# Top-k attention with a mixture of depths: the mask of each score tile is added by TensorE during the transpose, not by ScalarE and GpSimd ahead of it

## The chip, the cores and the metric

The kernel runs on one core of one Trainium2 chip. The metric is device time in microseconds (us) of one execution; smaller is better. A core has five engines that run their own queues in order and wait for each other by semaphores: PE (TensorE, matrix products; PEld is its loading of weights), DVE (VectorE), ACT (ScalarE), POOL (GpSimd) and SP, which here issues DMAs.

## The reference

For 8 batches and 8 heads, with 576 tokens and a head size of 64, attention keeps for each query the 32 largest scores of its 576, takes the softmax over them, and multiplies by the values. The result (8 x 576 x 512) goes through a mixture of depths: per batch a gate scores each token, and the 128 best tokens get a two-layer network added, scaled by a sigmoid.

```
scores = scale * np.matmul(q, k.transpose(0, 1, 3, 2))
kth = np.partition(scores, -top_k, axis=-1)[..., -top_k:-top_k + 1]
mask = scores >= kth
scores = np.where(mask, scores, -1000000000.0)
attn = np.exp(scores - max); attn = attn / (sum + 1e-09)
attn_out = np.matmul(attn, v)
...
top_idx = np.argpartition(-gate_scores[b], capacity)[:capacity]
out[b, top_idx] = x[b, top_idx] + sigmoid(gate)[:, None] * (relu(xe @ w1) @ w2)
```

## The kernel before

**Units and tiles.** The work is cut into 160 units: 8 batches, 5 blocks of queries (four of 128 rows, one of 64), 4 pairs of heads. A unit of a full block has two score tiles of 128 x 576, one for each head; a unit of the short block packs both heads into one tile. So each batch has 20 units and 36 tiles, and the run has 288 tiles.

**The pipeline.** One loop runs over steps n, one step for each unit, and a unit passes through six steps. In step n the engines do, for different units:

- PE: `turn` and `turn_last` of unit n-3 (transposes of the masked scores: four chunks of 128 x 128 for each tile, into the PSUM tile `ptr`, and one for the last 64 keys of both heads, into a corner of the score tile `ps`), between them `values` of unit n-4 (products with v into `av`), then `multiply` of unit n+1 (scores into `ps`), then a piece of the mixture of the batch before (`h_ps`, `y_ps`, `extra_ps`) or of loading the next batch (`tr`).
- DVE: `find_bound` of unit n (`cand`, `best`: a bound from the maxima of eight slices), then `find_kth` of unit n-1 (`next8`, shown as `next`: its element 7 is the 32nd largest score), then `gates` (`prod`) and parts of the mixture (`junk`, `sig`, `pick`).
- ACT: `part` of unit n-1 (`sides`, the sign of score minus bound), the exponentials of unit n-3 (`pT`, `last`), copies that were put off (`flush`), the first half of the mask of unit n-2 (`z`), `keep` of unit n+1 (`sc`, the scores copied out of PSUM), `keep_values` (`xs`), `cut` (the CAST to `seen`).
- POOL: `y` = score times side for unit n-1, `fill`, the second half of the mask of unit n-2 (`z`), once for each block of queries the normalisation `x`, and `lift` (`seen`, 2^90 times the 32nd largest score).

**Masking.** ACT makes z = relu(2^90 * (kth - score)) and POOL makes z = score - z, so that a score below the limit becomes hugely negative and its exponential is zero. Both are done for every tile:

```
act.activation(
    z[:, i, :],
    sc[:, i, :],
    AF.Relu,
    bias=seen[:, 1, at + i : at + i + 1],
    scale=-BIG,
)
pool.tensor_tensor(z[:, i, :], sc[:, i, :], z[:, i, :], ALU.subtract)
```

**What sets the order.** The order within each engine is that of the program, fixed by `InOrder` (its line, L42, is what the profile shows for all these instructions, so groups are told apart by their tiles). `ps` and `av` have one buffer each: `multiply` waits until ACT has read `last` from the corner of the same `ps`, and `values` waits until `keep_values` has emptied `av`. The masked tile `z` has two buffers, the scores `sc` four.

Of the kernel before, what the change touches and what calls it, by code (L numbers as in the profile page):

```python
# [20 lines left out]
BIG = 2.0**90  # L21
# [4 lines left out]
LEAST = 1.0e-16 * SMALLER  # L26
# [19 lines left out]
def kernel(  # L46
# [11 lines left out]
    nc = tc.nc  # L58
# [6 lines left out]
    JP = J * P  # L65
# [34 lines left out]
    slot = const.tile([P, CAP], FP32, name="slot")  # L100
    nc.vector.tensor_copy(out=slot, in_=slot_i)


# [239 lines left out]

    def lift(n, next8, at):
        pool.tensor_scalar_mul(seen[:, 1, at : at + n], next8[:, 0:n, 7], BIG)

    def turn(i, z):

        tr = ps_tr.tile([P, 512], FP32, name="ptr")
        for c in range(J):  # L350
            at = c * P + i * R
            pe.transpose(tr[:, c * P : (c + 1) * P], z[:, i, at : at + P], ident)
        return tr

    def turn_last(n, z, ps):

        last = z.rearrange("p i s -> p (i s)")[:, JP : JP + n * R]  # L360
        tr = ps[0 : n * R, 1, 1, 512 - P : 512]
        pe.transpose(tr, last, ident)
        return tr
# [91 lines left out]
    def break_ties(t, gate, gate_row, rank):  # L455

        n = R if t == J else P
        work = wkpool.tile([P, 2, S], FP32, name="ties", tag="z")
        tok_row = modpool.tile([P, S], I32, name="tok_row", tag="scratch")
# [183 lines left out]
    load_at = (1, 2, 3, 4, 7, 8, 9, 11, 12)  # L643
    first_load_at = (5, 6, 7, 8, 9, 10, 11, 12, 13)
    v_at = 6
    mix_from = 5
    first_tile, tiles = [], 0
# [10 lines left out]
    xs = x = gate = None  # L658
    scs, bests, zs, weights = {}, {}, {}, {}

    def tiles_of(n):
        return len(heads_of(units[n][1])) if 0 <= n < len(units) else 0

    for n in range(-1, len(units) + 6):
# [19 lines left out]
        for i in range(2):  # L684
            if i < tiles_of(n - 3):
                trs.append(turn(i, z))
                if i == tiles_of(n - 3) - 1:
                    trs.append(turn_last(i + 1, z, ps))
            if i < tiles_of(n - 4):
                values(t4, hp4, i, *weights[n - 4], av, qkv[b4][2])  # L690
# [6 lines left out]
        if tiles_of(n - 1):  # L697
# [21 lines left out]
        if tiles_of(n + 1):  # L719
            b, t, hp = units[n + 1]  # L720
            multiply(t, hp, *qkv[b][0:2], ps)


        if tiles_of(n - 2):
            sc = scs.pop(n - 2)
            z = wkpool.tile([P, 2, S], FP32, name="z")
            at = first_tile[n - 2]
            for i in range(tiles_of(n - 2)):
                act.activation(
                    z[:, i, :],  # L730
                    sc[:, i, :],
                    AF.Relu,
                    bias=seen[:, 1, at + i : at + i + 1],
                    scale=-BIG,
                )
# [15 lines left out]
        if gating is not None:  # L751
# [6 lines left out]
        b, i = divmod(n, per_batch)  # L758
        if i >= mix_from or b > 0:
            next(mixing, None)  # L760
        if normalising is not None:
# [9 lines left out]
        if tiles_of(n - 1):  # L771
            lift(tiles_of(n - 1), next8, first_tile[n - 1])
        b, i = divmod(n, per_batch)
        if n >= 0 and b + 1 < B:
            steps_of_load = first_load_at if b == 0 else load_at
            if i == steps_of_load[0] - 1:
                qkv[b + 1] = room_for_qkv(b + 1)
                loading = load_kq(k[b + 1], q[b + 1], *qkv[b + 1][0:2])
                next(loading)
            if i in steps_of_load:  # L780
                next(loading)
            if i == v_at:
                load_v(v[b + 1], qkv[b + 1][2])

# [7 lines left out]
    for what, op, than, limit in (  # L792
        (seen[:, 0, :], ALU.min, ALU.is_gt, LEAST),
        (seen[:, 1, :], ALU.min, ALU.is_gt, LEAST * BIG),
        (seen[:, 2, :], ALU.max, ALU.is_lt, float(MIDDLE)),
# [28 lines left out]
    def general_weights(n, sc):  # L824

        p = wkpool.tile([P, 2, S], FP32, name="p", tag="z")
        for i in range(n):
            cur, tops = sc[:, i, :], []
            left = wkpool.tile([P, 2, S], FP32, name="left", tag="z")
            for r in range(TOP_K // 8):  # L830
# [99 lines left out]
```

## Time and profile before

| | us |
|---|---|
| median of 3 runs | 1170.49 |
| lowest and highest of them | 1162.18, 1174.98 |
| the profiled execution | 1161.06 |
| its span in the trace | 1158.6 |

| engine | busy us | share of the span |
|---|---|---|
| PE | 985.9 | 85% |
| DVE | 910.0 | 79% |
| POOL | 905.8 | 78% |
| ACT | 879.7 | 76% |

The mean granted clock of PE is 0.878 of full speed. The four engines are nearly equally busy, so the shares alone say little; the sections below go by steps. Steps are counted here within a batch of 20, from 0 to 19, and a step is taken from one CAST of `cut` on ACT to the next. Batches are counted from 0; batch 4 lasts from 557.41 to 697.24 us.

### The profile page before, as it was taken

What the parts mean: (1) busy time and instruction counts of PE and PEld (TensorE: products, weight loads), DVE (VectorE), ACT (ScalarE), POOL (GpSimd) and SP (SyncE); (2) the same over time, 40 slices, a digit from 0 to 9 for tenths busy, and PEclk for the clock granted to TensorE, in tenths of its full rate; (3) what the DMA queues carried; (4) which work ended last, traced back from release to release, by engine and by line L of the source; (5) the groups of instructions that cost most, each with busy time, mean ns of one, the idle gap of its engine ahead of it and who ended that gap; (6) DMA issues with size and microseconds to landing.
All of it is one profiled execution on the core that took longest, in us unless ns stands there. A gap on an engine that the chain in (4) does not pass through costs nothing.

```text
span 1158.6 us, 23113 instructions
## 1 busy us (share of the span) xinstructions
PE 985.9 (85%) x6906; PEld 820.3 (71%) x6906; DVE 910.0 (79%) x4980; ACT 879.7 (76%) x2113; POOL 905.8 (78%) x974
## 2 busy tenths in 40 slices
PE   6788878899789988899888998889987898778946
PEld 3566657787677876778677786678766787667845
DVE  5888788787897778976898868978789777898640
ACT  4898798696978769777786878969797876978721
POOL 3999798797978769777787878879797887878820
PEclk9898897799977989779886899969998788978978
DMA  5641022100411013110141101410041001000020
GB/s 121 199 100 28 1 80 63 36 2 11 114 38 29 1 17 108 38 28 1 21 114 28 28 1 34 119 28 11 9 110 26 10 1 47 5 1 10 1 60 13
DMA packets 123829, 49.03 MB, mean 42 GB/s; under 512 B 118960, under 2 KB 118960, under 8 KB 122672
## 3 DMA queue, kind: packets, MB, share of 16 engines
q1 hardware_dynamic: 120320, 42.88, 14.4%
q0 software_dynamic: 1792, 4.20, 2.1%
q8 instruction: 58, 0.95, 0.3%
q14 instruction: 75, 0.61, 0.2%
q10 hardware_dynamic: 1584, 0.39, 0.2%
HBM read 35.91 MB, written 11.53 MB: 41 GB/s over the span
## 4 chain that ended last, share of the span: by engine, by line
PE 51%; ACT 20%; POOL 19%; DVE 5%; issue 4%; DMA 1%; POOLq 0%; ACTq 0%
PE av L42 18%; PE ps L42 13%; POOL y L42 9%; PE ptr L42 9%; POOL z L42 8%; PE h_ps L42 6%; ACT sides L42 6%; ACT sc L42 5%; PE y_ps L42 4%; ACT pT L42 3%; ACT z L42 3%; PE extra_ps L42 2%; DVE prod L42 1%; DVE next L42 1%; POOL out_dram L607 1%
## 5 line engine op out<-in xcount | busy, mean ns | idle before, releaser
L42 POOL TENSOR_TENSOR z<-sc,z 128x576 f32<-128x576 f32 x288 | 407.7, 1434 | 62.9 <-ACT z L42 61.9
L42 POOL TENSOR_TENSOR y<-sc,sides 128x576 f32<-128x576 f32 x288 | 363.0, 1279 | 116.9 <-ACT sides L42 109.1
L42 DVE MAX8 cand<-sc 128x8 f32<-128x72 f32 x2304 | 323.5, 216 | 89.9 <-ACT sc L42 89.4
L42 PE MATMUL av<-v,pT 128*128 128x65 f32 (+1 forms) x2560 | 340.9, 283 | 5.5 <-ACT xs L42 5.2
L42 PEld LDWEIGHTS av<-v,pT 128*128 128x128 f32 (+1 forms) x2560 | 324.2, 203 | 18.4 <-ACT xs L42 10.2
L42 PE MATMUL ptr<-ident,z 128*128 128x128 f32 x1152 | 206.5, 308 | 113.7 <-POOL z L42 113.7
L42 DVE MAX8 next<-y 128x8 f32<-128x584 f32 x288 | 207.8, 759 | 98.9 <-POOL y L42 97.6
L42 PE MATMUL ps<-kT,qT 64*128 64x288 f32 (+1 forms) x1280 | 232.4, 488 | 21.3 <-ACT last L42 16.6
L42 ACT COPY sc<-ps 128x576 f32<-128x576 f32 x288 | 171.7, 647 | 99.6 <-PE ps L42 99.5
L42 PEld LDWEIGHTS ptr<-ident,z 128*128 128x128 f32 x1152 | 146.0, 159 | 142.4 <-POOL z L42 139.1
L42 ACT ACTIVATE pT<-ptr 128x512 f32<-128x512 f32 x288 | 163.0, 585 | 88.4 <-PE ptr L42 87.8
L42 ACT ACTIVATE sides<-sc,seen 128x576 bf16<-128x576 f32 x288 | 221.1, 768 | 4.9
L42 ACT ACTIVATE z<-sc,seen 128x576 f32<-128x576 f32 x288 | 210.5, 783 | 1.4 <-POOL seen L42 1.4
L42 PEld LDWEIGHTS ps<-kT,qT 64*128 64x128 f32 (+1 forms) x1280 | 119.5, 203 | 73.2 <-ACT last L42 30.2
L42 DVE MAX8 best<-cand 128x8 f32<-128x64 f32 x864 | 154.2, 215 | 3.3
L42 DVE MATCH_REPLACE8 cand<-best,cand 128x64 f32<-128x64 f32 x576 | 116.5, 209 | 0.0
L42 PEld LDWEIGHTS h_ps<-xeT,w 128*128 128x128 f32 x512 | 64.7, 205 | 16.6 <-issue 11.8
L42 DVE CUSTOM_DVE_ANT_0 prod<-x,wg 128x512 f32<-128x512 f32 (+1 forms) x40 | 72.1, 1802 | 4.5 <-POOL x L42 4.5
L42 PE MATMUL h_ps<-xeT,w 128*128 128x128 f32 x512 | 70.9, 296 | 2.1 <-ACT hT L42 1.4
L42 PE MATMUL y_ps<-w,hT 128*128 128x192 f32 (+1 forms) x384 | 62.2, 315 | 1.5 <-ACT gy L42 1.1
L42 PE MATMUL av<-vpair,last 128*128 128x130 f32 x256 | 63.4, 333 | 0.0
L42 PEld LDWEIGHTS y_ps<-w,hT 128*128 128x128 f32 x384 | 56.1, 190 | 10.1 <-issue 7.7
(74 smaller groups left out, 859.3 us busy)
## 6 DMA issues: line engine op xcount, KB each, us to landing
rows<-in_k_dram SPq DMA_DIRECT2D x64, 128.0 KB, 2.8
v<-in_v_dram SPq DMA_DIRECT2D x64, 128.0 KB, 3.0
out_dram<-x SPq DMA_DIRECT2D x8, 1024.0 KB, 4.7
rows<-in_q_dram SPq DMA_DIRECT2D x62, 128.0 KB, 2.9
w<-in_moe_w_dram SPq DMA_DIRECT2D x2, 2048.0 KB, 14.0
last<-in_k_dram SPq DMA_DIRECT2D x8, 128.0 KB, 3.1
vlast<-in_v_dram SPq DMA_DIRECT2D x8, 128.0 KB, 3.7
vpair<-in_v_dram SPq DMA_DIRECT2D x16, 64.0 KB, 3.1
```

Of the source, the lines that this page charges most:

```text
L42: return lambda *a, **kw: self._tc.keep_in_program_order(fn(*a, **kw))
L607: nc.gpsimd.indirect_dma_start(out=out.flatten_outer_dims(), out_offset=bass.IndirectOffsetOnAxis(ap=row_i, axis=0), in_=gy, in_offset=Non ...
```

## The change

The scores themselves are now transposed, without a mask. After each transpose of a 128 x 128 chunk, TensorE adds to the same place in PSUM the product of a bf16 mask chunk `less` and a constant matrix `out_of_reach` (the identity times -2^90). `less` is positive (or 1) where a score lies below the 32nd largest and 0 elsewhere. Of the two tiles of a unit, ACT makes the mask of the first (a Relu) and POOL that of the second (a comparison); both read the limit from `next8`. `lift`, the product with 2^90, is gone; POOL copies the limits into `seen` for the check at the end. The scores must live longer, so `sc` has five buffers. The table of load steps is written in another form, for the same steps.

```diff
-    scpool = ctx.enter_context(tc.tile_pool(name="sc", bufs=4))
+    scpool = ctx.enter_context(tc.tile_pool(name="sc", bufs=5))
...
+    out_of_reach = const.tile([P, P], BF16, name="out_of_reach")
+    nc.vector.tensor_scalar_mul(out_of_reach, ident, -BIG)
...
-    def lift(n, next8, at):
-        pool.tensor_scalar_mul(seen[:, 1, at : at + n], next8[:, 0:n, 7], BIG)
-
-    def turn(i, z):
+    def mask(n, sc, next8):
+
+        less = wkpool.tile([P, 2, S], BF16, name="less")
+        for i in range(n):
+            kth = next8[:, i, 7:8]
+            if i == 0:
+                act.activation(less[:, i, :], sc[:, i, :], AF.Relu, bias=kth, scale=-1.0)
+            else:
+                pool.tensor_scalar(
+                    out=less[:, i, :],
+                    in0=sc[:, i, :],
+                    scalar1=kth,
+                    scalar2=None,
+                    op0=ALU.is_lt,
+                )
+        return less
+
+    def turn_some(tr, z, less):
+
+        pe.transpose(tr, z, ident)
+        if less is not None:
+            pe.matmul(
+                tr, less, out_of_reach, start=False, stop=True, skip_group_check=True
+            )
...
-            next8 = find_kth(tiles_of(n - 1), y)
+            next8s[n - 1] = find_kth(tiles_of(n - 1), y)
...
-            z = wkpool.tile([P, 2, S], FP32, name="z")
-            at = first_tile[n - 2]
-            for i in range(tiles_of(n - 2)):
-                act.activation(
...
-                pool.tensor_tensor(z[:, i, :], sc[:, i, :], z[:, i, :], ALU.subtract)
-            zs[n - 2] = z
+            w, at = tiles_of(n - 2), first_tile[n - 2]
+            kth = next8s.pop(n - 2)
+            masks[n - 2] = mask(w, scs[n - 2], kth)
+            pool.tensor_copy(out=seen[:, 1, at : at + w], in_=kth[:, 0:w, 7])
```

The order of the instructions on PE, in a step with full units early in the run. In the kernel before, `ptr` and the first `ps` row are `turn` and `turn_last`, the two `av` rows `values`, the last `ps` row `multiply`:

```order
L42 MATMUL ptr<-ident,z 128x128 x4
L42 MATMUL av<-v_115,pT 128x65 x4
L42 MATMUL ptr<-ident,z 128x128 x4
L42 MATMUL ps<-ident,z 128x128
L42 MATMUL av<-v_115,pT 128x65 x4
L42 MATMUL av<-vpair_119,last 128x130
L42 MATMUL ps<-kT,qT 128x288 x4
```

The transposes stand where they stood; each is now followed by one loading of `less` and one product.

On PE after the change, from the last chunk of the second `turn` of such a step to its `multiply` (the first three rows stand three more times ahead of these):

```order
L42 MATMUL ptr<-ident,sc 128x128
L42 LDWEIGHTS less
L42 MATMUL ptr<-out_of_reach,less 128x128
L42 MATMUL ps<-ident,sc 128x128
L42 LDWEIGHTS less
L42 MATMUL ps<-out_of_reach,less 128x128
L42 MATMUL av<-v_117,pT 128x65 x4
L42 MATMUL av<-vpair_121,last 128x130
L42 MATMUL ps<-kT,qT 128x288 x4
```

A full unit has nine such pairs, a unit of the short block five; none existed before.

On POOL before the change, over a step at whose end a block of queries is normalised (`x`), and into the next:

```order
L42 TENSOR_TENSOR y<-sc,sides 128x576 x2
L42 TENSOR_TENSOR y<-steps,seen 128x2x8
L42 TENSOR_TENSOR z<-sc,z 128x576 x2
L42 TENSOR_TENSOR x<-xs,rden 128x512
L42 TENSOR_SCALAR seen<-next_908 128x2
L42 TENSOR_TENSOR y<-sc,sides 128x576 x2
```

Here `lift` (the `seen` row) stands behind `x`, and the mask of the next step needs it.

On POOL after the change, the same place:

```order
L42 TENSOR_TENSOR y<-sc,sides 128x576 x2
L42 TENSOR_TENSOR y<-steps,seen 128x2x8
L42 TENSOR_SCALAR less<-sc,next_853 128x576
L42 COPY seen<-next_853 128x2
L42 TENSOR_TENSOR x<-xs,rden 128x512
L42 TENSOR_TENSOR y<-sc,sides 128x576 x2
```

Two subtractions became one comparison, and what stands behind `x` is no longer needed by any mask.

## Rows read from the trace of the kernel before

**Rows 1.** The page: POOL's two costliest groups (busy us, mean ns, idle before).

```profile
L42 POOL TENSOR_TENSOR z<-sc,z 128x576 f32<-128x576 f32 x288 | 407.7, 1434 | 62.9 <-ACT z L42 61.9
L42 POOL TENSOR_TENSOR y<-sc,sides 128x576 f32<-128x576 f32 x288 | 363.0, 1279 | 116.9 <-ACT sides L42 109.1
```

**Rows 2.** Stretches of batch 4: length, busy PE, PEld, DVE, ACT, POOL, PEclk, DMA.

```profile
562.84:578.64 15.80, 12.16 (x80) 8.80 (x81) 13.14 (x70) 11.90 (x31) 12.35 (x14) 0.78 0.21 34
578.64:590.47 11.83, 9.93 (x78) 8.09 (x76) 9.38 (x63) 11.77 (x29) 11.44 (x13) 1.00 0.53 165
590.47:605.57 15.10, 12.81 (x78) 10.93 (x79) 15.03 (x75) 11.79 (x30) 13.77 (x15) 0.77 0.33 74
617.41:638.89 21.48, 19.30 (x87) 16.66 (x88) 15.79 (x86) 12.13 (x32) 15.28 (x16) 0.54 0.06 14
650.73:665.80 15.07, 14.42 (x93) 12.38 (x94) 12.85 (x69) 11.63 (x28) 12.09 (x13) 0.77 0.00 1
665.80:690.99 25.19, 25.19 (x204) 22.27 (x203) 15.80 (x73) 18.15 (x45) 19.41 (x23) 1.00 0.01 1
```

**Rows 3.** The same columns: two stretches of batch 5, one of batch 0, whole batches.

```profile
728.96:741.41 12.45, 9.49 (x75) 8.03 (x75) 12.45 (x68) 11.78 (x29) 12.12 (x13) 1.00 0.40 90
788.79:800.68 11.89, 11.25 (x93) 9.87 (x94) 11.89 (x68) 11.41 (x28) 11.56 (x13) 1.00 0.00 0
106.72:124.09 17.37, 16.98 (x74) 13.44 (x74) 10.90 (x54) 10.21 (x25) 13.94 (x15) 0.51 0.00 1
...
143.98:970.55 826.57, 730.99 (x5173) 612.11 (x5172) 676.82 (x3723) 656.77 (x1584) 673.25 (x714) 0.88 0.16 39
970.55:1097.15 126.60, 107.56 (x760) 90.51 (x759) 108.52 (x584) 100.28 (x243) 107.53 (x115) 0.88 0.05 15
```

**Rows 4.** Timeline of one plain step (batch 4, step 3), ACT: start, length, what.

```profile
577.43 1.19 ACT L42 COPY sc<-ps 128x576 f32<-128x576 f32 x2
578.48 0.27 ACT L42 COPY xs<-av 64x130 f32<-64x130 f32 x1
...
581.37 0.27 ACT L42 ACTIVATE last<-ps 128x128 f32<-128x128 f32 x1
...
582.00 1.45 ACT L42 ACTIVATE z<-sc,seen 128x576 f32<-128x576 f32 x2
583.33 0.65 ACT L42 COPY sc<-ps 128x576 f32<-128x576 f32 x1
```

**Rows 5.** The same step: weight loads of PE; its last product, of `multiply`.

```profile
578.42 0.42 PEld L42 LDWEIGHTS ptr<-ident,z 128*128 128x128 f32 x4 [1.04 <-POOL z L42]
578.80 0.97 PEld L42 LDWEIGHTS av<-v,pT 128*128 128x128 f32 x8
579.78 0.42 PEld L42 LDWEIGHTS ptr<-ident,z 128*128 128x128 f32 x4
580.17 0.14 PEld L42 LDWEIGHTS ps<-ident,z 128*128 128x128 f32 x1
580.28 0.97 PEld L42 LDWEIGHTS av<-v,pT 128*128 128x128 f32 x8
581.17 0.30 PEld L42 LDWEIGHTS av<-vpair,last 128*128 128x128 f32 x2
...
581.69 1.24 PE L42 MATMUL ps<-kT,qT 64*128 64x288 f32 x8
```

**Rows 6.** Timeline of batch 4, step 1, and of the tail (1104.27): DVE, PE.

```profile
562.73 2.41 DVE L42 CUSTOM_DVE_ANT_0 prod<-x,wg 128x512 f32<-128x512 f32 x1
...
564.64 1.11 PE L42 MATMUL ptr<-ident,z 128*128 128x128 f32 x4 [2.58 <-POOL z L42]
...
1104.27 0.69 DVE L42 CUSTOM_DVE_ANT_0 prod<-x,wg 128x512 f32<-128x512 f32 x1 [3.27 <-POOL x L42]
```

**Rows 7.** Timeline of batch 4, step 9, ACT.

```profile
620.52 0.20 ACT L42 ACTIVATE sig<-sig 128x4 f32<-128x4 f32 x1 [2.87 <-DVE sig L42]
```

**Rows 8.** Timeline of batch 4, step 2: weight loads of 64 columns.

```profile
572.54 0.54 PEld L42 LDWEIGHTS av<-v,pT 128*64 128x64 f32 x8 [0.53 <-ACT xs L42]
```

More of the change, by code (lines that the diff above doesn't have):

```diff
@@ L342, in find_kth, with turn, turn_last @@
         return next8
-    def lift(n, next8, at):
-        pool.tensor_scalar_mul(seen[:, 1, at : at + n], next8[:, 0:n, 7], BIG)
-    def turn(i, z):
+    def mask(n, sc, next8):
[19 more added lines that the diff above has]
+            )
+    def turn(i, z, less=None):
         tr = ps_tr.tile([P, 512], FP32, name="ptr")
         for c in range(J):
-            at = c * P + i * R
-            pe.transpose(tr[:, c * P : (c + 1) * P], z[:, i, at : at + P], ident)
-        return tr
-    def turn_last(n, z, ps):
-        last = z.rearrange("p i s -> p (i s)")[:, JP : JP + n * R]
+            at = slice(c * P + i * R, (c + 1) * P + i * R)
+            turn_some(
+                tr[:, c * P : (c + 1) * P],
+                z[:, i, at],
+                None if less is None else less[:, i, at],
+            )
+        return tr
+    def turn_last(n, z, ps, less=None):
         tr = ps[0 : n * R, 1, 1, 512 - P : 512]
-        pe.transpose(tr, last, ident)
+        last = [
+            a and a.rearrange("p i s -> p (i s)")[:, JP : JP + n * R] for a in (z, less)
+        ]
+        turn_some(tr, *last)
         return tr
@@ L457, in break_ties @@
         n = R if t == J else P
-        work = wkpool.tile([P, 2, S], FP32, name="ties", tag="z")
+        work = wkpool.tile([P, 2, S], FP32, name="ties", tag="y")
         tok_row = modpool.tile([P, S], I32, name="tok_row", tag="scratch")
@@ L644 @@
     first_load_at = (5, 6, 7, 8, 9, 10, 11, 12, 13)
+    load_steps = {}
+    for b in range(B - 1):
+        at = [b * per_batch + i for i in (load_at if b else first_load_at)]
+        load_steps[at[0] - 1] = b + 1, True
+        load_steps.update({n: (b + 1, False) for n in at})
     v_at = 6
-    mix_from = 5
     first_tile, tiles = [], 0
@@ L658 @@
     xs = x = gate = None
-    scs, bests, zs, weights = {}, {}, {}, {}
+    scs, bests, next8s, masks, weights = {}, {}, {}, {}, {}
     def tiles_of(n):
@@ L685 @@
             if i < tiles_of(n - 3):
-                trs.append(turn(i, z))
+                trs.append(turn(i, sc, less))
                 if i == tiles_of(n - 3) - 1:
-                    trs.append(turn_last(i + 1, z, ps))
+                    trs.append(turn_last(i + 1, sc, ps, less))
             if i < tiles_of(n - 4):
@@ L770 @@
                 normalising = b, t, xs, x, gate
-        if tiles_of(n - 1):
-            lift(tiles_of(n - 1), next8, first_tile[n - 1])
-        b, i = divmod(n, per_batch)
[L774 to L783, printed above, removed]
+        if n in load_steps:
+            b, begin = load_steps[n]
+            if begin:
+                qkv[b] = room_for_qkv(b)
+                loading = load_kq(k[b], q[b], *qkv[b][0:2])
+            next(loading)
+        b, i = divmod(n, per_batch)
+        if i == v_at and b + 1 < B:
+            load_v(v[b + 1], qkv[b + 1][2])
     flush()
@@ L793 @@
         (seen[:, 0, :], ALU.min, ALU.is_gt, LEAST),
-        (seen[:, 1, :], ALU.min, ALU.is_gt, LEAST * BIG),
+        (seen[:, 1, :], ALU.min, ALU.is_gt, LEAST),
         (seen[:, 2, :], ALU.max, ALU.is_lt, float(MIDDLE)),
```

17 lines of the change are left out of this document (4 added, 13 removed).

## The prediction

> **What bounds the kernel now.** I read the page first. Its busy shares are so even that no engine bounds the whole, so I went through batch 4 step by step with the view of busy time by stretch [rows 2]. Four kinds of steps stand out.
>
> Plain steps: steps 3 and 4 take 11.83 us together, and ACT is busy for 11.77 of them, POOL for 11.44 [rows 2] (from 578.64). Steps 7-8 and 11-12 read the same (11.84 each). The timeline says why [rows 4]: from one `keep` (577.43) to the next (583.33) ACT never pauses. POOL is as full, with two `y` and two `z`, 1.28 and 1.43 us each on the mean [rows 1].
>
> PE-full steps: in steps 15 to 18 PE is busy for all of 25.19 us, at a granted clock of 1.00 [rows 2] (from 665.80). There the mixture runs on PE beside attention.
>
> Slow pairs: steps 1-2 (15.80 us), 5-6 (15.10) and 13-14 (15.07), with a mean granted clock of 0.77 to 0.78 [rows 2]. The timeline of step 1 shows the cause [rows 6]: DVE's `prod` takes 2.41 us beside POOL's `z` (0.69 in the tail, where POOL is idle), and PE stands 2.58 us waiting for `z`. After that the clock is at its lower level, and the next products take twice as long. That the work itself doesn't need the time is seen in batch 5, where the same two pairs kept the full clock and took 12.45 and 11.89 [rows 3].
>
> The pair 9-10: 21.48 us, at a clock of 0.54 [rows 2] (from 617.41). Here ACT waits 2.87 us for DVE's `sig` [rows 7] and all else waits for ACT; then PE works through the backlog at half speed.
>
> **Removed.** POOL loses two `z` of 1.43 us for each full unit [rows 1], ACT one of its two (a pair takes 1.45 us with overlap, and from the first one's start to `keep` is 1.33, so one is worth 0.67) [rows 4]. `lift` becomes a copy of the same size, and nobody waits for it. PE's wait for `z` ahead of `turn` (1.04 us even in the plain step [rows 5], 2.58 in the slow one [rows 6]) goes: the first tile's mask comes from ACT, which made it a step earlier, right behind the flushed copy.
>
> **Added on POOL.** One comparison of 128 x 576. No row shows one. It can't be cheaper than nothing, and a two-input `z`, 1.43 us, is the upper end; I take 1.0, since it reads one tensor instead of two. POOL then has about 2.5 for `y`, 1.0, and some 0.5 for small ones: 4.0 in a step of 5.7. PE needs this mask only for its second `turn` of the next step, nearly two microseconds after POOL has it. So either end is hidden; the cover is gone only if POOL is about 1.8 us late.
>
> **Added on PE.** Nine pairs of a load of `less` and a product of 128 columns for a full unit, five for a short one: 128 x 9 + 32 x 5 = 1312. Call the price of one pair x. No row shows a bf16 product. Nearest rows: the fp32 transposes, four in 0.39 us (579.78 to 580.17), so 0.0975 each; products with 128 columns of fp32 weights, eight in 0.97, so 0.121 [rows 5]; with 64 columns, as many bytes as 128 of bf16, eight in 0.54 of loading, 0.068 [rows 8]. Below, I allow half a transpose, 0.049. I take x = 0.08, between the 64-column load and the transpose.
>
> [...]
>
> **What is late next in a plain step.** Two loops remain. Through ACT: `keep` starts, `last` starts 3.94 later (577.43 to 581.37), `multiply` 0.32 after that, and the next `keep` needs all its 1.24 us and a handover of some 0.06: 5.56 [rows 4, 5]. ACT's mask and flushed copy fit beside `multiply`. Through PE: `values` can start 1.37 after `keep` starts, because `xs` must have emptied `av` (578.80); from there to the end of the last `av` load is 2.67 (581.47), then `multiply`, 1.30: 5.34. Five of the nine new pairs lie in this part, the other four in PE's gap before `xs`. So the step takes 5.34 + 5x = 5.74, against 5.92 now.
>
> **The sum for batch 4**, in us, before to after:
> Steps 3-4 and 11-12: 11.83 to 11.5, twice: -0.7.
> Steps 1-2: 15.80 to 11.6, two plain steps, one with only five pairs: -4.2. PE no longer stands still for `z`, so I expect the clock to stay up, and `prod` meets an idle POOL.
> Steps 5-6: 15.10 to 11.6: -3.5. The undisturbed 12.45 was DVE-full [rows 3], with perhaps 0.9 of it `prod` waiting behind POOL (up to 1.7 by [rows 6]).
> Steps 13-14: 15.07 to 12.0: -3.1, from the undisturbed 11.89, less the wait of `prod`, plus nine pairs in a PE-full step.
> Steps 7-8: 11.84 to 12.5: +0.65. DVE has five `junk` products there, which now fall into faster steps.
> Steps 15-18, PE-full: 36 pairs: +2.9. Steps 19 and 0: ten pairs: +0.8.
> Steps 9-10: `sig` stays; about 0.9 less for `prod`, nine pairs at half clock (2x): +0.5.
> Together -6.65, from 139.83 to 133.2.
>
> Batches 1 to 6 take 826.57 now [rows 3], some of them with fewer slow pairs. If each comes to 133.2, that is 799: -27.5. Batch 0 has two steps at half clock, 17.37 us [rows 3], which should become 11.6, and plain steps: -9. Batch 7, 126.60 [rows 3], has three slow pairs, no loading and half of the PE-full steps: -6. In the tail PE waits for three last `z`: -3. Sum -45.5.
>
> The profiled execution took 1161.06, so 1115.5; it was 0.8% below the median of 1170.49, and the forecast on the median's scale is 1115.5 x 1.008 = 1124. In the batches x counts some 123 times (50 in loops, 73 in PE-full and half-clock steps), over the run about 920 times. So 0.01 in x is 9 us, and the gain is gone at x = 0.129.
>
> **Rival 1, still faster: the clock stays up in steps 9-10 too.** PE has more to do in every step and no longer starts that pair with a wait for `z`. Without the half clock the pair would take about 16.9 instead of 22.0, seven times: 36 us less, 1088 on the median's scale. Against it: PE was busy for 19.30 of 21.48 us there and still was at half clock [rows 2], and the stall of ACT for `sig`, which starves PE, remains. [...]
>
> **Rival 2, no gain: the new pairs are dear.** If a bf16 load costs what the fp32 load costs, x = 0.121 [rows 5], 38 us of the gain go: 1153, on the median's scale 1163, within 1% of now. For it: nothing in the trace shows a cheaper load of 128 columns than a transpose. [...]
>
> **Rival 3, slower: the halved clock stays in the slow pairs.** PE's waits may only move, from ahead of `turn` to ahead of `multiply`: `prod`, `junk` and the normalisation keep DVE full there (15.03 of 15.10 us [rows 2]), and PE still waits for `last`. Then each pair keeps its 15 us and pays nine pairs at double price: about 3.9 us back for each of some 20 slow pairs of the run, 78 us: 1194, on the median's scale 1203. It decides from about 12 of the 20. For it: DVE's work is unchanged. Against it: each slow pair begins with a wait for `z`, and that is gone.
>
> **How the numbers follow.** Forecast, 1095 to 1150 (x from 0.05 to 0.0975, on the median's scale): 0.55. Rival 1: 0.17. Rival 2: 0.15. Rival 3: 0.13. The range reaches from a little below rival 1 to above rival 2: 1080 to 1168. About 1% is what a measurement of this kernel can tell from no change. Faster by more: forecast, rival 1 and a part of rival 2, 0.76; within 1%: most of rival 2, 0.11; slower: rival 3, 0.13.
>
> **What would show it.** Right: in a plain step PE goes from `multiply` into `turn` without a wait, and its idle time is ahead of `av`, ended by `xs`; plain steps last 5.7; steps 15 to 18 lengthen to about 28; the clock is 1.00 in steps 1-2, 5-6, 13-14; POOL's busy time falls to about 620 us, ACT's by about 90. The pitch of the pairs in `turn` gives x directly. Wrong: a pitch above 0.12, half clock in the slow pairs, or a `turn` that waits for POOL's `less`.

## The result, and the profile after

The changed kernel takes 1092.52 us (median of 4 runs, 1090.8 to 1094.8), the kernel before 1170.36 (4 runs, 1162.18 to 1174.98): a ratio of 0.9343, 95% interval 0.9288 to 0.9399. The profiled execution took 1090.8 us, its span is 1088.9.

The page: busy time, the chain that ended last, and the groups that answer to [rows 1] (busy us, mean ns, idle before).

```profile
PE 996.2 (91%) x8218; PEld 828.7 (76%) x8218; DVE 854.4 (78%) x4981; ACT 799.8 (73%) x1985; POOL 706.0 (65%) x814
...
PE 69%; ACT 18%; POOL 5%; issue 4%; DVE 3%; DMA 1%; SPq 0%; ACTq 0%; POOLq 0%
...
L42 POOL TENSOR_TENSOR y<-sc,sides 128x576 f32<-128x576 f32 x288 | 363.4, 1280 | 287.8 <-ACT sides L42 287.8
...
L42 PE MATMUL ptr<-out_of_reach,less 128*128 128x128 bf16 x1152 | 220.9, 225 | 13.3 <-POOL less L42 13.3
L42 POOL TENSOR_SCALAR less<-sc,next 128x576 bf16<-128x576 f32 x128 | 220.9, 1726 | 0.0
...
L42 PEld LDWEIGHTS <-less 128*128 128x128 bf16 (+1 forms) x1312 | 141.1, 108 | 19.6 <-POOL less L42 14.9
```

PE is now the busiest engine by a distance, and POOL has become an engine that waits: 287.8 us of idle time ahead of `y`. The mean granted clock rose from 0.878 to 0.942. PE waits for POOL's mask only 13.3 us in the whole run.

Batch 3, by the stretches of [rows 2] (steps 1-2, 3-4, 5-6, 7-8, 9-10, 13-14, 15-18; steps 11-12 read like 5-6), then batches 1 to 6 and batch 7, which answer to [rows 3]. The columns are the same.

```profile
395.41:406.71 11.30, 9.88 (x93) 7.37 (x92) 11.16 (x70) 10.51 (x28) 9.28 (x11) 1.00 0.28 47
406.71:418.19 11.48, 11.13 (x96) 9.27 (x96) 10.24 (x64) 10.68 (x27) 9.68 (x10) 1.00 0.52 165
418.19:429.69 11.50, 10.74 (x93) 8.98 (x93) 11.05 (x68) 10.32 (x27) 9.59 (x12) 1.00 0.46 103
429.69:442.51 12.82, 12.26 (x106) 10.30 (x105) 12.66 (x74) 10.95 (x27) 8.25 (x10) 1.00 0.31 70
442.51:461.75 19.24, 16.41 (x95) 13.39 (x93) 14.88 (x86) 10.75 (x28) 12.31 (x14) 0.65 0.08 16
...
473.25:485.18 11.93, 11.74 (x104) 10.20 (x104) 10.66 (x67) 10.08 (x26) 9.45 (x11) 1.00 0.01 2
485.18:512.94 27.76, 27.76 (x236) 24.26 (x235) 15.08 (x73) 17.00 (x43) 11.99 (x16) 1.00 0.00 1
...
130.68:908.44 777.76, 736.60 (x6150) 617.32 (x6151) 636.00 (x3722) 597.48 (x1489) 523.43 (x594) 0.95 0.17 41
908.44:1029.43 120.99, 110.58 (x919) 92.00 (x918) 100.74 (x584) 89.92 (x226) 84.75 (x95) 0.94 0.06 16
```

The three slow pairs are gone: 1-2, 5-6 and 13-14 have the full clock and last 11.3 to 11.9 us, where batch 4 had 15.07 to 15.80. Steps 15 to 18 pay for it with 2.57 us (25.19 to 27.76). From batch 1 on only the pair 9-10 still has the lower clock, in each of the seven batches; batch 0 has it in steps 1-2 (13.30 us at 0.50). Batches 1 to 6 lost 48.8 us of their 826.57, batch 0 11.8 (124.37 to 112.58, by its step boundaries), batch 7 5.6, and start and tail together 3.5: that is the difference of the spans, 69.7 us.

A plain step of the changed kernel (batch 3, from one `keep` to the next; timeline: start, length, what), to be read beside [rows 4, 5]:

```profile
416.97 1.18 ACT L42 COPY sc<-ps 128x576 f32<-128x576 f32 x2 [0.31 <-PE ps L42]
...
417.34 0.27 PE L42 MATMUL ptr<-ident,sc 128*128 128x128 f32 x1
417.45 0.22 PE L42 MATMUL ptr<-out_of_reach,less 128*128 128x128 bf16 x1
...
417.85 0.28 PE L42 MATMUL ptr<-ident,sc 128*128 128x128 f32 x1
417.96 0.22 PE L42 MATMUL ptr<-out_of_reach,less 128*128 128x128 bf16 x1
418.37 1.11 PE L42 MATMUL av<-v,pT 128*128 128x65 f32 x8 [0.19 <-ACT xs L42]
...
421.44 1.24 PE L42 MATMUL ps<-kT,qT 64*128 64x288 f32 x8
...
422.72 1.18 ACT L42 COPY sc<-ps 128x576 f32<-128x576 f32 x2 [0.31 <-PE tr L42]
```

From `keep` to `values` is 1.40 us, from there to `multiply` 3.07, from there to the next `keep` 1.28: together 5.75. The first and the fourth transpose of `turn` start 0.51 apart, so transpose and pair take 0.17; with the 0.0975 for a transpose of [rows 5] that leaves 0.072 for the pair. The 0.39 us in which [rows 5] has four loads are a little short, since the first of them starts early (0.06 ahead of the second, the others 0.11 apart): two transposes in a row start 0.109 apart (the median in steps 15 to 18 of the kernel before), which leaves 0.061 between them. PE's idle time stands ahead of `av` and ends with `xs`.

The start of step 9 in batch 3 (timeline of POOL, DVE, ACT and PE):

```profile
438.61 0.20 DVE L42 RECIPROCAL rden<-sums 128x8 f32<-128x8 f32 x1
438.90 1.04 POOL L42 TENSOR_TENSOR x<-xs,rden 128x512 f32<-128x512 f32 x1 [3.35 <-DVE rden L42]
...
442.57 1.73 POOL L42 TENSOR_SCALAR less<-sc,next 128x576 bf16<-128x576 f32 x1
...
443.99 0.67 DVE L42 CUSTOM_DVE_ANT_0 prod<-x,wg 128x512 f32<-128x512 f32 x1
...
444.36 0.29 PE L42 MATMUL ptr<-out_of_reach,less 128*128 128x128 bf16 x1 [1.72 <-POOL less L42]
...
444.86 0.21 ACT L42 ACTIVATE sig<-sig 128x4 f32<-128x4 f32 x1 [2.14 <-DVE sig L42]
...
446.39 0.20 ACT L42 ACTIVATE sig<-sig 64x1 f32<-64x1 f32 x1 [1.32 <-DVE sig L42]
...
449.28 2.29 PE L42 MATMUL ps<-kT,qT 64*128 64x288 f32 x8 [1.11 <-ACT last L42]
```

Two stalls follow one another. DVE makes `rden` only behind its `junk` comparisons, POOL holds back `x`, `y` and `less` for it, and PE stands 1.72 us. Then ACT stands 2.14 and 1.32 us for `sig`. The view by stretch says where the clock is in this:

```profile
442.51:443.78 1.27, 0.13 (x2) 0.00 (x0) 1.15 (x2) 0.19 (x1) 1.27 (x2) 1.00 0.62 139
443.78:457.43 13.65, 11.97 (x57) 9.97 (x58) 12.15 (x79) 7.86 (x20) 8.71 (x11) 0.50 0.01 1
457.43:461.75 4.32, 4.32 (x38) 3.42 (x36) 1.59 (x7) 2.70 (x7) 2.34 (x3) 1.00 0.14 27
```

It fell to its lower level, 0.50, while PE stood for `less`, and stayed there for 13.65 us.

### The profile page after: what moved, and what is told of

Its sections match the earlier page's. It is cut to its first block, busy times and chain, and to the rows that moved or that the text cites. A ratio compares the mean times of both kernels' runs of the same rounds, so it can differ in the third digit from the quotient of the medians.

```text
span 1088.9 us, 25441 instructions
## 1 busy us (share of the span) xinstructions
PE 996.2 (91%) x8218; PEld 828.7 (76%) x8218; DVE 854.4 (78%) x4981; ACT 799.8 (73%) x1985; POOL 706.0 (65%) x814
## 4 chain that ended last, share of the span: by engine, by line
PE 69%; ACT 18%; POOL 5%; issue 4%; DVE 3%; DMA 1%; SPq 0%; ACTq 0%; POOLq 0%
PE av L42 25%; PE ps L42 18%; PE ptr L42 11%; ACT sc L42 9%; PE h_ps L42 6%; PE y_ps L42 6%; POOL y L42 3%; ACT sides L42 3%; PE extra_ps L42 2%; ACT pT L42 2%; ACT xs L42 1%; POOL less L42 1%; DVE next L42 1%; ACT kT L42 1%; DVE pick L42 1%
## 5 line engine op out<-in xcount | busy, mean ns | idle before, releaser
L42 POOL TENSOR_TENSOR y<-sc,sides 128x576 f32<-128x576 f32 x288 | 363.4, 1280 | 287.8 <-ACT sides L42 287.8
L42 PE MATMUL av<-v,pT 128*128 128x65 f32 (+1 forms) x2560 | 327.8, 273 | 23.9 <-ACT xs L42 23.6
L42 PEld LDWEIGHTS av<-v,pT 128*128 128x128 f32 (+1 forms) x2560 | 294.2, 187 | 50.1 <-ACT xs L42 44.8
L42 PE MATMUL ptr<-ident,sc 128*128 128x128 f32 x1152 | 241.4, 289 | 0.0
L42 PE MATMUL ptr<-out_of_reach,less 128*128 128x128 bf16 x1152 | 220.9, 225 | 13.3 <-POOL less L42 13.3
L42 PE MATMUL ps<-kT,qT 64*128 64x288 f32 (+1 forms) x1280 | 207.0, 444 | 22.0 <-ACT last L42 19.1
L42 POOL TENSOR_SCALAR less<-sc,next 128x576 bf16<-128x576 f32 x128 | 220.9, 1726 | 0.0
L42 PEld LDWEIGHTS ptr<-ident,sc 128*128 128x128 f32 x1152 | 174.7, 152 | 24.3 <-issue 10.0
L42 PEld LDWEIGHTS <-less 128*128 128x128 bf16 (+1 forms) x1312 | 141.1, 108 | 19.6 <-POOL less L42 14.9
L42 ACT ACTIVATE less<-sc,next 128x576 bf16<-128x576 f32 x160 | 125.7, 785 | 0.0
L42 POOL TENSOR_TENSOR x<-xs,rden 128x512 f32<-128x512 f32 (+1 forms) x40 | 41.7, 1042 | 44.2 <-DVE rden L42 44.2
```

The source lines that it names most:

```text
L42: return lambda *a, **kw: self._tc.keep_in_program_order(fn(*a, **kw))
```

## The experiments

Each ratio below is to the kernel before, run beside the experiment on the same chip. The experiments ran on three chips, where the kernel before took 1161.5, 1163.4 and 1169.3 us (medians of 7); the changed kernel itself was not run again there. Steps of equal work repeat across the traces (steps 15 to 18 take 27.75 us in seven of them), so the experiments are also compared with it step by step, in microseconds.

**What a pair costs.** Each product of the mask is issued twice.

```diff
-            pe.matmul(
-                tr, less, out_of_reach, start=False, stop=True, skip_group_check=True
-            )
+            for _ in range(2):
+                pe.matmul(
+                    tr, less, out_of_reach, start=False, stop=True, skip_group_check=True
+                )
```

> The changed kernel, with each product of the mask issued twice (a second load of less and a second product; the output does not change, since a key out of reach is only pushed out twice as far). It measures the price x of one pair. The pitch seen in the changed kernel is 0.17 us for transpose and pair together, which leaves 0.072 for the pair. If that is the price, steps 15 to 18 lengthen by 36 x 0.072 = 2.6 us, from 27.7 to 30.3, plain steps by 5 to 9 pairs (5.75 to 6.1 or 6.4), a batch by some 130 x 0.072 = 9 us, the run from 1092 to about 1158. Rival 1 (the first product hides in the shadow of the next load, and only a second one shows its full price, that of an fp32 load, 0.12): steps 15 to 18 come to 32, the run to over 1190. Rival 2 (it is the additional work on TensorE that keeps the clock up): the half clock in steps 9-10, 13.65 us in each batch now, gets shorter or goes, and the run stays under 1130.

1135.18 us (1134.34 to 1136.73), ratio 0.9753 (0.9682 to 0.9824). Steps 5-6 and 15 to 17 of batch 3, then steps 15 to 17 of the changed kernel:

```profile
434.11:446.18 12.07, 11.71 (x113) 10.06 (x112) 10.98 (x67) 10.32 (x27) 9.13 (x11) 1.00 0.42 94
...
503.96:525.56 21.60, 21.60 (x208) 18.98 (x207) 11.35 (x54) 12.94 (x34) 10.40 (x13) 1.00 0.00 1
...
485.18:505.27 20.09, 20.09 (x181) 17.47 (x180) 11.34 (x54) 12.97 (x33) 10.42 (x13) 1.00 0.01 2
```

In steps 15 to 17, PE-full to the end, 27 more pairs took 1.51 us: 0.056 each, half of the 0.109 of a transpose, and less than the 0.072 that I expected. (Steps 15 to 18 together take 29.54, only 1.78 more: in step 18 the CAST that ends it gained on PE, whose own products came 0.51 later there too.) A first pair, between two transposes, costs a step more (0.071, by the next run) than a second one behind its like. A plain step got 0.285 longer, about five pairs: as many as stand between `values` and `multiply`. Rival 1 is out. The clock still fell in steps 9-10 of every batch, for 6.8 to 10.2 us instead of 13.65; as PE's wait for `less` was shorter there too (0.90 us in batch 3), the run doesn't say whether the work kept it up.

**No product at all.** The masks are made, and nothing reads them.

```diff
         pe.transpose(tr, z, ident)
-        if less is not None:
-            pe.matmul(
-                tr, less, out_of_reach, start=False, stop=True, skip_group_check=True
-            )
```

> The changed kernel without the products of the mask: ACT and POOL make the masks as before, but nothing reads them, so that the softmax goes over all 576 scores (this part of the computation is left out). It tells what keeps the clock up in steps 1-2, 5-6 and 13-14. Theory: that TensorE no longer waits there for POOL's z. Then the clock stays at 1.00 in these pairs without the new products too, steps 15 to 18 fall from 27.7 to 25.2, plain steps from 5.75 to about 5.5, and the run comes to some 1045 us (1030 to 1060). Rival: the new products, as additional work, keep the clock up. Then half clock returns in most of these pairs, they take 14 to 15 us again, some 20 of them cost 3 us each, and the run comes to 1090 or more.

The whole run takes 4847.8 us and says nothing by itself: the softmax now goes over all 576 scores, its sums leave the bounds within which the kernel trusts its fast path, and behind it the general path computes everything again. What counts is the part before that, batches 1 to 6. They take 757.7 us by their step boundaries, 20.1 less than in the changed kernel. Batch 3: steps 1-2, 5-6, 9-10, 13-14, 15-18; and PE in step 9.

```profile
387.03:398.09 11.06, 9.06 (x78) 6.64 (x78) 11.06 (x71) 10.50 (x29) 9.54 (x11) 1.00 0.29 48
409.34:420.60 11.26, 9.69 (x75) 7.95 (x75) 10.88 (x67) 10.32 (x27) 9.42 (x11) 1.00 0.49 110
433.55:454.26 20.71, 15.61 (x76) 12.89 (x74) 14.84 (x86) 10.77 (x29) 12.32 (x14) 0.67 0.08 21
465.53:476.68 11.15, 10.81 (x89) 9.37 (x90) 10.79 (x67) 10.07 (x27) 9.33 (x11) 1.00 0.00 1
476.68:501.88 25.20, 25.20 (x204) 22.27 (x203) 15.07 (x74) 16.87 (x44) 12.34 (x18) 1.00 0.00 1
```

```profile
440.31 2.29 PE L42 MATMUL ps<-kT,qT 64*128 64x288 f32 x8 [5.10 <-ACT last L42]
```

The three pairs keep the full clock without the new products: it isn't the added work that holds it up. Steps 15 to 18 are back at 25.20, so a pair costs 2.56 / 36 = 0.071 there. Plain steps take 5.63, 0.12 less than with nine pairs. And steps 9-10 are longer without the products, 20.71 (18.66 in batch 1): PE now gets through `turn` at full speed, and stands 5.10 us for ACT, which stands for `sig`. I had expected 1045 for the run; the six batches point to some 1070.

**The wait alone.** The kernel before, with the turning and the product with v a step later; the loads and the mixture move a step along with them, and all else stays.

```diff
-        if tiles_of(n - 3):
+        if tiles_of(n - 4):
...
-            z, trs = zs.pop(n - 3), []
+            z, trs = zs.pop(n - 4), []
-        if tiles_of(n - 4):
-            b4, t4, hp4 = units[n - 4]
+        if tiles_of(n - 5):
+            b4, t4, hp4 = units[n - 5]
...
```

> The kernel before, in which only the turning and the product with v come one step later (units n-4 and n-5 instead of n-3 and n-4, the loads and the mixture shifted with them, z in its two buffers): TensorE finds z a step old, but POOL and ACT do all their old work and there is no product of a mask. Theory: the wait for z with the clock that falls behind it was the larger part of the gain. Then steps 1-2, 5-6 and 13-14 go from 15 to about 12 us, steps 15 to 18 stay at 25.2, a batch takes 130 to 133 us instead of 138, the run 1100 to 1125. Rival: the gain came from the load taken off POOL and ACT (prod waits beside POOL, and ACT is full). Then the pairs stay at 14 us or more, and the run stays within 1.5% of 1170.

1134.61 us (1129.2 to 1139.25), ratio 0.9764 (0.969 to 0.9837). Batch 3: steps 1-2, 5-6, 13-14, and `prod` in steps 5-6.

```profile
406.58:419.44 12.86, 10.44 (x100) 8.10 (x98) 12.14 (x62) 11.21 (x29) 12.13 (x13) 1.00 0.25 40
432.04:444.25 12.21, 9.83 (x76) 8.09 (x77) 10.66 (x65) 11.95 (x29) 11.88 (x13) 1.00 0.78 219
...
491.95:504.18 12.23, 11.03 (x88) 9.28 (x89) 10.70 (x66) 11.42 (x29) 11.92 (x13) 1.00 0.10 22
...
438.61 1.88 DVE L42 CUSTOM_DVE_ANT_0 prod<-x,wg 64x512 f32<-64x512 f32 x1
```

With the same work on POOL and ACT and without any product, the three pairs have the full clock and lost 8.7 us together against [rows 2] (15.80, 15.10 and 15.07 in batch 4 there). PE waits for POOL in none of them in batches 1 to 7, while `prod` still runs into POOL's `z` (1.9 us, in steps 1-2 mostly 3.8). So the wait for `z`, with the clock behind it, was the cause of these pairs, and not the slow `prod` by itself. The wait doesn't always bring the half clock: in steps 5-6 of the kernel before PE waited 1.67 and 1.65 us in batch 5, 1.68 and 1.65 in batch 4, and only batch 4 lost the clock. But batch 3 takes 134.06 us, a little more than I expected, and the run 10 us more, because the half clock of 9-10 now runs on into 11-12 (16.3). In batches 1 to 6 this kernel gains 23.5 us of the 48.8 that the change gains. That the rest came with the load taken off POOL and ACT is likely; no run tests it alone.

**The two stalls of step 9.** First `sig` alone: its exponential comes in the mixture's first step.

```diff
-        yield from route(gate, rank, exact)
-        yield
...
-            act.activation(sig[0:n, t0:t1], sig[0:n, t0:t1], AF.Exp, scale=-1.0)
+            def sigmoid(s=sig[0:n, t0:t1]):
+                act.activation(s, s, AF.Exp, scale=-1.0)
+
+            late.append(sigmoid)
+        yield from route(gate, rank, exact)
+        yield
+        for t0, t1, n in parts:
```

> The changed kernel, in which the exponential for sig (DVE's preparation and ACT's part) comes in the mixture's first step instead of behind the choice of tokens, so that ACT finds DVE's sig ready in steps 9-10, where it now waits about 2 us. It tests the pair that I had forecast worst (22.0 us, measured 19.24), and whether ACT's wait for sig is what brings the half clock there. Theory: without that wait the clock stays up or falls later, steps 9-10 take 13 to 16 us instead of 19.2, seven times, and the run comes to 1055 to 1075. Rival 1: the clock falls there for another cause (DVE's choice of tokens fills the pair, and best comes late for ACT's cut and so for sides and next); then the pair stays within 1 us of 19.2 and the run within 1% of 1092. Rival 2: moved work collides with the first step's DVE work, and a slow pair arises there instead: no change in the sum.

1094.26 us (1084.91 to 1095.69), ratio 0.9377 (0.9297 to 0.9456): no gain. ACT's waits for `sig` are gone, and steps 9-10 take 20.1 to 20.7 us in batches 1 to 5, but 17.30 and 15.45 in batches 6 and 7. Both my theory and the cause that I gave its rival were wrong: PE still stood for POOL, and DVE's `pick` ran into POOL's `y`.

```profile
448.64 0.29 PE L42 MATMUL ptr<-out_of_reach,less 128*128 128x128 bf16 x1 [1.72 <-POOL less L42]
...
449.17 3.28 DVE L42 TENSOR_SCALAR pick<-slot,ranks 128x128 f32<-128x128 f32 x4
...
841.60:858.90 17.30, 15.58 (x94) 12.84 (x93) 16.58 (x82) 10.58 (x26) 12.04 (x14) 0.70 0.00 1
```

The last line is the pair in batch 6. PE stood 1.72 us for `less` in all seven batches, and the clock fell in all seven, but it stayed down for 17.1 to 20.5 us in the first five, for 10.2 in batch 6 and for 6.8 in batch 7. What sets this length I can't say.

So a second theory: two stalls, each enough by itself. Next, `rden` alone, ahead of the comparisons. In the order of DVE that is the only difference, once in each batch.

```
 L42 MAX next_2797<-y 128x8 x2
+L42 TENSOR_SCALAR sums<-xs 128x8
+L42 RECIPROCAL rden<-sums 128x8
 L42 TENSOR_SCALAR junk,ranks<-gate_row,gate 128x576
 L42 TENSOR_SCALAR junk,ranks<-gate_row,gate 64x576
-L42 TENSOR_SCALAR sums<-xs 128x8
-L42 RECIPROCAL rden<-sums 128x8
```

> The changed kernel, in which one pair of DVE's instructions changes its place once per batch: sums and rden (the normalisation) stand ahead of the two junk comparisons of step 8 and not behind them. In the changed kernel POOL's x waits for rden (from 435.55 to 438.90), y and less shift behind it, and TensorE stands 1.72 us for POOL's less at 444.36, where the clock falls. Theory of two stalls (each by itself brings the half clock in steps 9-10: this one, and ACT's wait for sig of 2.14 and 1.32 us right behind it): the wait for less goes or falls under 0.3 us, but TensorE then runs out of work before ACT has sig and stands about 5 us ahead of multiply, as in the run without the mask's products (5.10); the half clock of 13.65 us stays, steps 9-10 take 18.5 to 21 us, and the run stays within 1% of 1092. Rival: the wait for less alone brings the half clock. Then steps 9-10 fall to 16 us or less, and the run to 1070 or less.

1091.83 us (1090.22 to 1094.68), ratio 0.9403 (0.9339 to 0.9466): as the two stalls foretold, no gain. The wait for `less` is under 0.3 us, steps 9-10 take 19.09 to 19.21 us in all seven batches, and PE stands for ACT:

```profile
450.27 1.33 PE L42 MATMUL ps<-kT,qT 64*128 64x288 f32 x4 [4.18 <-ACT last L42]
```

Then both moves together.

> The changed kernel with both moves: sums and rden ahead of the junk comparisons of step 8, and the exponential for sig in the mixture's first step (which alone left the run at 1094). Theory of two stalls: with both gone TensorE has no wait over 0.5 us in steps 9-10, the clock stays up or falls late, the pair takes 13 to 16 us instead of 19.3, seven times: 1050 to 1072. Rival (DVE's work in the pair, next, prod and the pick products, which took 3.28 us beside POOL's y in the run with sig moved, makes cut and sides late all the same): half clock of 10 us or more in most batches, pair 18 us or more, run 1080 to 1095.

1078.56 us (1073.41 to 1085.46), ratio 0.9305 (0.9236 to 0.9373), 13.3 us less than with `rden` alone on the same chip. Each move alone gave nothing, both together do: the four runs with both lie below all four with `rden` alone. (By the ratio alone this kernel, 0.9305, can't be told from the changed one, 0.9343.) The gain is smaller than I expected, and the run lies between the two ranges: steps 9-10 take 15.2 to 17.4 us. PE has no wait over 0.77 us in them, and the clock still falls in all seven batches, later and mostly for less long (3.4 to 13.7 us). So the two stalls are not all that brings it down. Batch 3:

```profile
437.33:443.51 6.18, 4.63 (x36) 3.58 (x35) 6.11 (x16) 5.45 (x13) 5.20 (x7) 1.00 0.11 26
443.51:450.34 6.83, 6.74 (x36) 6.14 (x36) 6.83 (x50) 3.30 (x10) 2.18 (x3) 0.50 0.01 2
```

DVE is full in both stretches. Its four large `pick` products took 2.24 us beside POOL's `y` (0.84 in the changed kernel, where POOL stood still), and ACT waited 3.87 us for `best`.

**Who makes which mask.** Both on ACT (`if i >= 0`), both on POOL (`if i < 0`), and the two changed over (`if i == n - 1`):

```diff
         for i in range(n):
             kth = next8[:, i, 7:8]
-            if i == 0:
+            if i >= 0:
```

> The changed kernel with both masks of a unit on ACT and none on POOL. POOL's comparison takes 1.73 us, a good deal more than the 1.0 that I had taken for it, ACT's Relu 0.68 to 0.78. If POOL's comparison costs nothing in plain steps, as the forecast had it (POOL is idle 1.2 us a step, waiting for sides), taking it away gains nothing there, and ACT's additional 0.7 us a step must fit beside multiply: behind the exponentials ACT waits 0.2 to 0.3 us for ps, so some 0.4 us of it are left over, and plain steps go from 5.75 to 5.9 to 6.2; steps 15 to 18, bound by TensorE, stay at 27.75. TensorE's wait for POOL's less ahead of steps 9-10 goes. Sum: 12 plain or loading steps of 20 at +0.3, 7 batches: 1100 to 1125. Rival: ACT's second mask hides, and the wait for less was what brought the half clock: 1060 to 1085.

1124.23 us (1119.28 to 1124.95), ratio 0.9664 (0.9597 to 0.973). Pairs of plain steps take 11.77 to 12.30, steps 15 to 18 the same 27.75, the wait for POOL is gone, and steps 9-10 of batches 1 to 6 take 21.4 to 22.2. The run lies in the theory's range, but not only for its reason: of the 30.8 us that batches 1 to 6 lose against the changed kernel, 15.7 lie in steps 9-10, of which it said nothing. The rival is out: without any wait for `less` the half clock stays there.

> The changed kernel with both masks of a unit on POOL and none on ACT. It asks how much cover POOL's comparison has, which came out at 1.73 us and not at 1.0. POOL then has in a plain step 2.5 for y, 0.2 for fill, 2 x 1.73 and 0.2 to 0.45 for the copy: 6.4 to 6.6, over the 5.75 that the step takes now, and once every four steps x of 1.04 more. Theory: POOL becomes the bound of plain and loading steps (6.5 to 6.8 us each, pairs 13 to 14), steps 15 to 18 keep 27.75, TensorE waits for less in every plain step and the clock falls in some: 1150 to 1230. Rival: POOL's comparison is slow only beside work of DVE and gets shorter, or ACT freed by 0.8 us a step gives it back: within 2% of 1092.

1195.76 us (1183.93 to 1213.62), ratio 1.0166 (1.0086 to 1.0246). POOL's comparison doesn't get shorter:

```profile
L42 POOL TENSOR_SCALAR less<-sc,next 128x576 bf16<-128x576 f32 x288 | 504.4, 1781 | 0.0
```

Nor is it slow only beside DVE: seven of the 288 fell where DVE did nothing, and took 1.71 to 1.73 us. PE waits 100.3 us for it, pairs of steps up to 14 (but for 9-10) take 12.0 to 17.0, and all that the change had won is gone.

> The changed kernel with the two masks changed over: POOL makes that of the first tile and ACT that of the second. In a plain step of the changed kernel POOL has its mask at 418.43, TensorE starts the first product of the first turn at 417.45 and that of the second at 419.43. So the first turn now waits about 0.9 us for POOL, values come 0.6 later, and as a longer step gives POOL's mask the same time more, plain steps settle at about +0.3: 5.75 to 6.0, some 12 of 20 steps, steps 15 to 18 stay at 27.75. Theory (the forecast's: it is ACT's mask in front and the 1.8 us behind it that hide POOL's): 1112 to 1130, and 1140 if the clock falls in further pairs. Rival (TensorE's slack ahead of values, which waits for xs anyway, covers it): within 1% of 1092.

1110.94 us (1101.21 to 1130.9), ratio 0.9456 (0.9382 to 0.9531).

```profile
L42 PE MATMUL ptr<-out_of_reach,less 128*128 128x128 bf16 x1152 | 219.6, 225 | 67.2 <-POOL less L42 66.6
...
455.86:473.19 17.33, 15.41 (x108) 12.78 (x109) 14.79 (x86) 10.63 (x28) 11.47 (x14) 0.80 0.07 16
```

The wait for POOL rose from 13.3 to 66.6 us, plain steps from 5.75 to 5.94 (I had 6.0). So the order matters by 1.7%: PE needs the first tile's mask before POOL can have it. Steps 9-10 (the last line, batch 3) took 17.3 us in five batches and over 23 in two, which I can't explain: both stalls are there in all seven, PE's for `less` even longer (2.95 to 3.39 us), ACT's for `sig` as before (2.1 and 1.3).

**Four buffers of scores** (`bufs=4` for `sc`).

> The changed kernel with four buffers of scores instead of five. Scores of a unit live from keep (step n-1 for unit n) until the turn of step n+3; with four buffers keep of unit n+1 in step n overwrites the scores of unit n-3, which that step's turn reads ahead of its multiply. Since multiply stands behind that turn on TensorE, keep would come after it anyway. Theory: the fifth buffer costs and gains nothing, the run stays within 0.5% of 1092. Rival: keep has to wait for the end of turn and of POOL's or ACT's reading, a step later each time: more than 1% slower, 1105 or more.

1105.9 us (1102.8 to 1108.78), ratio 0.9528 (0.9464 to 0.9592). My theory missed: the fifth buffer is worth about 1%. No instruction changes its place, but `keep` now also waits for POOL, which read the same buffer for its mask a step earlier. In a plain step that wait has long been met when `multiply` starts:

```profile
424.02 1.24 PE L42 MATMUL ps<-kT,qT 64*128 64x288 f32 x8
...
425.36 1.18 ACT L42 COPY sc<-ps 128x576 f32<-128x576 f32 x2 [0.43 <-PE ps L42]
```

Still `keep` starts 1.34 us behind `multiply`, where it was 1.28, and plain pairs take 11.62 for 11.50: some 3 us over the 26 of them. The rest is mostly in steps 9-10 (18.6 to 21.9), whose length changes from batch to batch in other runs too; that it is the buffer's doing there is not shown.

**Where a product costs its full price.** Units 12 to 17 of each batch from the second on, which are turned beside the mixture, are masked by subtraction again.

```diff
+    def subtract(n, sc, lifted):
+
+        less = wkpool.tile([P, 2, S], BF16, name="less")
+        for i in range(n):
+            act.activation(
+                less[:, i, :], sc[:, i, :], AF.Relu, bias=lifted[:, i : i + 1], scale=-BIG
+            )
+            pool.tensor_tensor(sc[:, i, :], sc[:, i, :], less[:, i, :], ALU.subtract)
+        return sc
...
+            if n - 2 in by_subtraction:
+                scs[n - 2] = subtract(w, scs[n - 2], lifteds.pop(n - 2))
+                masks[n - 2] = None
```

> The changed kernel, in which the units turned in the TensorE-full steps (units 12 to 17 of each batch from the second on) are masked by subtraction again: POOL's lift, ACT's Relu into less, POOL's score minus less in place, and a turn without products. It tests that in steps 15 to 18 the pairs are paid in full and nothing else is, and whether the wait for POOL's z was harmless there. Theory: steps 15 to 18 fall from 27.76 to 25.2, the neighbouring TensorE-full steps by up to 1 us, a batch by 2.6 to 3.6 us, the run to 1068 to 1076. Rival (the wait of turn for POOL returns, as it did in steps 13-14 of the kernel before, and brings the half clock): a pair of 15 us in each batch and 1085 or more.

1068.76 us (1066.53 to 1078.18), ratio 0.9161 (0.9103 to 0.922). Steps 13-14 and 15 to 18 of batch 3:

```profile
465.86:477.13 11.27, 11.09 (x94) 9.66 (x95) 10.45 (x66) 11.14 (x28) 10.09 (x14) 1.00 0.00 1
477.13:502.33 25.20, 25.20 (x204) 22.27 (x203) 15.94 (x74) 18.16 (x45) 18.85 (x27) 1.00 0.01 2
```

The products are gone from the steps in which nothing hides them, and the subtraction is harmless there.

**All three moves in one kernel.**

> The three moves that have an effect in one kernel: units 12 to 17 of each batch masked by subtraction, the exponential for sig in the mixture's first step, and sums and rden ahead of the junk comparisons (the last two alone gave 1078.6). Theory: the gains lie in different steps (15 to 18 and 9-10) and add up: 1054 to 1064. Rival: one of them brings a wait into the other's steps (POOL's subtractions ahead of TensorE's turn of steps 14 and 15): 1072 or more.

1055.35 us (1045.68 to 1057.76), ratio 0.8999 (0.8936 to 0.9062): the moves add up (steps 15 to 18 take 25.2 us, steps 9-10 16.3 to 17.4), 13.4 us less than with the subtraction alone on the same chip, and this kernel is faster than the kernel before and the changed one.

## Why the prediction was right, and where it was off

The forecast was 1124 us, a gain of 4.0%; measured were 1092.5, 6.6%, inside the range. Its mechanism held; one term of the sum was mis-sized.

**The slow pairs** went as forecast: 11.30, 11.50 and 11.93 for 11.6, 11.6 and 12.0. That PE's wait for `z` was their cause is shown by the kernel before with a later `turn`, where `prod` was as slow as ever; that the products aren't needed for the full clock, by the run without them. `prod` is as short as I had supposed, 0.67 us in place of 2.41 [rows 6], a mean of 673 ns for all 40 where it was 1802. But POOL isn't idle beside it: 31 of the 40 overlap a `less`, and none takes more than 0.69 us. In the kernel before, the 37 that overlap a `z` took 1.20 to 2.42, the other three 0.67 to 0.69. So `prod` is slow beside the subtraction and not beside the comparison; why, no run shows.

**x** was taken as 0.08 and is 0.071 in steps 15 to 18 (25.20 to 27.76 for 36 pairs). In the plain step the five pairs between `values` and `multiply` took 0.40 (2.67 to 3.07), just as reckoned: 5.75 us for 5.74. That ACT's loop stands close behind shows in the run without products: 5.63, where I had 5.56. Steps 7-8, full of DVE's `junk`, came to 12.82 for 12.5. Rival 2 (0.121) is out. One reading of [rows 5] was loose: the 0.0975 and 0.121 are spans of loads, where the products start 0.109 and 0.111 apart. That a pair costs 0.071 and 0.056, less than the 108 ns of the profile's row for its load, is no contradiction: 1258 of the 1312 loads of `less` start before the load ahead of them has ended. Why the pair is cheaper than a transpose, no run shows.

**POOL's comparison** was taken as 1.0 us, with 1.43 as its upper end. It takes 1.73: a wrong bound, which cost nothing in plain steps because the cover was there. It is also why POOL's busy time fell to 706 us and not to 620. How much cover: in the plain step the mask is ready at 418.43 and the second `turn` reads it at 419.43, so 1.0 us is left of the 1.8 that were forecast; with POOL's mask in front the run gets 1.7% slower, with both on POOL the gain is gone.

**Steps 9-10** are the step of the prediction that failed: 22.0 forecast, 19.24 measured (18.62 to 19.49 in batches 1 to 6). That makes 16.7 of the 21.4 us by which batches 1 to 6 beat their 799. I had kept the half clock at its old length and added nine pairs at double price (the two steps hold eighteen). It was shorter: from [rows 2], 21.48 x 2 x (1 - 0.54) = 19.8 us before, and 13.65 after (6.8 in batch 4). The prediction saw ACT's wait for `sig`; it missed that PE's wait for POOL stays there too, now for `less`, since `rden` stands behind `junk`; a `turn` that waits for `less` was one of its own signs of being wrong, and here it came true (1.72 us). The runs show that ACT's wait for `sig`, with less than 0.2 us for `less`, goes with a pair of 18.7 to 22.2 us in every batch from 1 on (no products, both masks on ACT, `rden` moved), that the wait for `less` without the one for `sig` does so in five batches of seven, and that with neither the pair takes 15.2 to 17.4. That is less than a cause: with the masks changed over both waits are there, and five pairs of seven take 17.3. Within a run the pair gets longer with its time at half clock (`sig` moved: 15.45 us with 6.8, 17.30 with 10.2, 20.1 to 20.7 with 17.1 to 20.5), and that time is not the same behind the same wait. So why the clock came back some six microseconds sooner than before stays open: removing one stall made that stretch mostly longer (`sig`, 17.1 to 20.5 us in five batches of seven) or shorter (`rden`, 10.24 in batch 3).

**The scale** was the second, smaller miss: I multiplied by 1.008, since the profiled execution was that far below its median. The changed kernel's own is 0.16% below, so the excess wasn't a proportion of the time: about 7 of the 31.5 us between forecast and result. Batch 0 gave 11.8 us for 9; batch 7 and the tail 5.6 and 2.0 for 6 and 3.

**Rival 1** (1088) is nearer to the measured time than the forecast, but not by its mechanism: the clock fell in steps 9-10 of all seven batches. What it named against itself, the stall for `sig`, is still there. **Rival 3** is out: PE's waits didn't move to `multiply` (for `last` it waits 19.1 us in the whole run, 16.6 before).

## What to carry to other kernels

Work that is moved to the busiest engine can pay if it ends a wait of that engine: look for what the engine does behind the wait (here at half the clock), and move the work only to steps in which something else ends last. Where a stretch stays slow after one wait in it is removed, look for the second one before giving the first move up; two moves that do nothing alone were worth 1.2% together here. Look at every batch before a cause is named: one batch of seven, or two, can read otherwise. A new operation's cover is a number to be read off the timeline, from the end of the operation to the first reader.

## What the hardware showed that I had not expected

- POOL's comparison with a limit for each partition, one input, bf16 out, takes 1.73 us for 128 x 576; its subtraction of two inputs takes 1.43 [rows 1].
- A second load and product of bf16 right behind its like costs 0.056 us, the first behind an fp32 transpose 0.071.
- Behind the same wait of 1.72 us TensorE's clock stayed at its lower level for 6.8 to 20.5 us, in seven batches of one run (`sig` moved).
- DVE's four `pick` products, one tensor and one value for each partition each, take 0.84 us beside an idle POOL and 3.28 beside its `y` and `less` (`sig` moved).
- A copy on ACT that waits for two engines instead of one starts 0.06 us later, though the second wait has long been met (1.34 us behind `multiply` for 1.28). That the second wait is the cause is read off the two traces, no run tests it apart.
